# A two-part kernel with its MLP started later, its weight conversion moved with it, and a reordered first stage

## The chip, the cores and the metric

The kernel runs on one core of a Trainium2 chip. A core has five engines with a queue each, worked off in order: TensorE (PE; PEld are its weight loads), VectorE (DVE), ScalarE (ACT), GpSimd (POOL) and SyncE (SP, which here only issues transfers). The metric is the device time of one execution in microseconds, the median of several runs. The profile is of one further execution.

## The reference

Two computations in a row. The first is attention by random features, over 8 batches of 8 heads with 576 positions of 64 numbers:

```python
def phi(x):                                   # q and k, scaled by 64 ** -0.25
    proj = np.einsum('bhsd,md->bhsm', x, omega)          # omega: 128 x 64
    h = proj - np.sum(x * x, axis=-1, keepdims=True) / 2.0
    h = h - np.max(h, axis=-1, keepdims=True)
    return np.exp(h) / np.sqrt(m)
kv = np.einsum('bhsm,bhsd->bhmd', k_p, v)
num = np.einsum('bhsm,bhmd->bhsd', q_p, kv)
den = np.einsum('bhsm,bhm->bhs', q_p, np.sum(k_p, axis=2))[..., None] + 1e-06
```

Its result, as 4608 rows of 512, goes through a gated MLP, `silu(x @ w_gate) * (x @ w_val) @ w_out`, with 1536 inner columns. The three weights come in double precision (two 32-bit words a number).

## The kernel before, in words

Attention runs in 72 steps. A step takes two groups of 256 positions of a pair of heads: six steps with two groups of k (`AHEAD = 6`), then a q group and a k group each, and at the end two q groups. For a step, SP loads the two groups (`nat`), TensorE transposes them (`pt`), ScalarE copies them to SBUF (`x`, one copy a step, issued a step ahead), TensorE projects them on omega (`pp`), POOL squares them (`sq`), and VectorE forms the row sums of the squares and the row maxima of `pp` (`st`) and from both, in two small instructions, the bias of the exponential that ScalarE takes (`ph`). Groups of k are then multiplied with v into `kvacc`. Groups of q are transposed once more (`ptq`), multiplied with the sums (`po`), normalised (`xn`) and transposed (`xt`); ScalarE and VectorE split the result into a high and a low part, `xh` and `xl`, the MLP's input. `po`, `xt` and `ptq` share one PSUM buffer in most of the program, so that `xl` must be done before the next of them is written. `pt` takes PSUM from the MLP's pool of four buffers in the steps before `DENSE` and that single buffer from then on.

The MLP works on ten tiles of columns (512 wide, the first and last 256) and four sets of three blocks of 128 inner columns. A visit to one tile with one set is 36 gate matmuls (`g`), 36 value matmuls (`v`, both line 641), then 9 matmuls (`o`, line 650) for every 128 columns. All are products of high and low parts, three for one. Tiles are grouped in rounds, and the first round visits three tiles with all four sets.

A planner lays the MLP's work between the attention steps. `whole` tells after which step a tile is complete, `upper` and `lower` bound how many planned microseconds of MLP may and must be given out by a step, and `course` is the straightest line between. In step n the loop calls eleven pieces of attention work (`ORDER`) and after each gives out MLP matmuls (`give`) until `course` is met. What it writes down in this order, a scheduler then orders on each engine by its own estimate.

The weights are converted on the chip, in 36 pieces of 128 x 512 numbers. `convert_all` is a generator with seven operations a piece: ScalarE (L260), five on VectorE (L262, L264, L266, L268, L270), POOL's closing add (L272) with the store of the piece to a scratch tensor in HBM (`wscr`). `load_raw` (L225, L230) brings a piece's raw words into one of two buffers; a buffer is free again when the add has read it. The loop calls `tick` for one operation, as often as `want` says, which `marks` set: pairs of a step and a number of pieces. Before the change these are steps 0, 21, 23, 30, 33 and 35 with 0, 6, 9, 18, 27 and 36 pieces. The pieces of the first set stay in SBUF as high and low parts (`whi`, `wlo`), and later sets are read back from `wscr` and split when their set begins.

Of the kernel before, what the change touches and what calls it, by code (L numbers as in the profile page):

```python
# [16 lines left out]
ALU = mybir.AluOpType  # L17
AX = mybir.AxisListType
# [5 lines left out]
def kernel(  # L24
# [11 lines left out]
    nc = tc.nc  # L36
    B, H, S, D = q.shape
    M = omega.shape[0]
# [7 lines left out]
    NF = DF // P  # L46
# [3 lines left out]
    FA = 3  # L50
    NSET = NF // FA
# [8 lines left out]
    ROUNDS = [range(0, 3), range(3, 5), range(5, 7), range(7, 10)]  # L60
# [52 lines left out]
    AHEAD = 6  # L113
# [17 lines left out]
    def column(b, gr):  # L131
        return b * S + (S - RES if gr is None else gr[1])
# [50 lines left out]
    upper, lower = np.zeros(NN + 1), np.zeros(NN + 1)  # L183
    for n in range(NN + 1):
        vi = 0
        while vi < len(visits) and whole[visits[vi][0]] < n:
            vi += 1
        upper[n] = cum[vi] if n > whole[1] else 0.0
        lower[n] = max([0.0] + [cum[last_visit[j - NXB] + 1] for j in begun if j >= NXB and begun[j] <= n])
    lower = np.minimum(lower, upper)  # L190
    course = (lower + upper) / 2
# [23 lines left out]
    wscr = dram.tile([NF, 3, P, DM], F32, name="wscr")  # L215
    raws = {}

    def load_raw(n):
        if n < 3 * NF:
            f, i = divmod(n, 3) if n >= 3 * FA else (n % FA, n // FA)  # L220
            w = (wg32, wv32, wo32)[i]
            raw = att.tile([P, 2 * DM], I32, name=f"st{f}_{i}", tag="stw")
            raws[n] = f, i, raw
            if i < 2:
                nc.sync.dma_start(  # L225
                    raw.rearrange("p (c f) -> p c f", f=2 * P),
                    w[:, f * 2 * P : (f + 1) * 2 * P].rearrange("(c p) f -> p c f", p=P),
                )
            else:
                nc.sync.dma_start(raw, w[f * P : (f + 1) * P, :])  # L230
# [16 lines left out]
    def convert_all():  # L247


        load_raw(0)  # L250
        for n in range(3 * NF):
            load_raw(n + 1)
            f, i, raw = raws.pop(n)
            if f < FA:
                new_weights(f, i)
            u = moe.tile([P, DM], F32, name=f"wc{f}_{i}", tag="wraw", bufs=3)
            pairs = raw.rearrange("p (n t) -> p n t", t=2)
            low, r = pairs[:, :, 0], pairs[:, :, 1].bitcast(F32)
            ri, ui = r.bitcast(I32), u.bitcast(I32)
            nc.scalar.activation(u, r, AF.Abs)  # L260
            yield
            nc.vector.tensor_scalar(u, u, E_LO, E_HI, op0=ALU.max, op1=ALU.min)  # L262
# [3 lines left out]
            nc.vector.scalar_tensor_tensor(ri, ri, -0x40000000, ui, op0=ALU.bitwise_and, op1=ALU.bitwise_or)  # L266
# [3 lines left out]
            nc.vector.scalar_tensor_tensor(u, low.bitcast(U32), 2.0**-52, u, op0=ALU.mult, op1=ALU.mult)  # L270
            yield
            nc.gpsimd.tensor_tensor(u, r, u, op=ALU.add)  # L272
            if f < FA:
                split_piece(f, i, u)
            nc.sync.dma_start(wscr[f, i], u)
            converted.add((f, i))
            yield

# [43 lines left out]
    nats = {}  # L322
    busy = []

    def load_group(t, src, b, gr, v_):
        if gr is not None:
            pr, r = gr
            nc.sync.dma_start(
                t[:, :, :, 0:D],
                src[b, 2 * pr : 2 * pr + 2, r : r + G, :].rearrange("h (p c) d -> p c h d", c=CH),  # L330
            )
            return
        for c in range(CH):
            for j, pr in enumerate(pairs_of(gr)[c]):
                nc.sync.dma_start(
                    t[j * RES : (j + 1) * RES, 2 * c + j if v_ else c, :, 0:D],
                    src[b, 2 * pr : 2 * pr + 2, S - RES : S, :].rearrange("h p d -> p h d"),
                )

    def load(n):  # L340
        if n >= NS:
            return
        nats[n] = att.tile([P, 2, CH, 2, D], F32, name=f"nat{n}", tag="nat", bufs=3)
# [4 lines left out]
    def load_v(n):  # L348
        for i, b, g, gr in slots(n, "k"):
            rest = gr is None  # L350
            ts = (vtile, vrest)[rest]
            t = ts[nv[rest] % len(ts)]
            nv[rest] += 1
            assert t not in busy, "v's tile is still needed"
            busy.append(t)
            vrows[b, g] = t
            load_group(t, v, b, gr, True)

    box = {}
    sts = {}  # L360
# [38 lines left out]
    def st_max(n):  # L399
        if n >= NS:  # L400
            return
        st, sq, pp = sts[n]

        nc.vector.tensor_reduce(
            st[:, 0].rearrange("p i c h -> p (i c h)"),
            sq.rearrange("p i c h d -> p (i c h) d"),
            axis=AX.X,
            op=ALU.add,
        )
        for hh in range(2):  # L410
            nc.vector.tensor_reduce(st[:, 1, :, :, hh], pp[hh], axis=AX.X, op=ALU.max, negate=True)  # L411
        s0, s1, s2, s3 = (st[:, j].rearrange("p i c h -> p (i c h)") for j in range(4))
        nc.vector.scalar_tensor_tensor(s2, s0, SQC, s1, op0=ALU.mult, op1=ALU.add)
        nc.vector.scalar_tensor_tensor(s3, s0, -SQC, s2, op0=ALU.mult, op1=ALU.add)  # L414
        return True
# [405 lines left out]
```

## Time and profile before

| | |
|---|---|
| median of 3 runs | 1260.99 us (1258.11 to 1264.03) |
| the profiled execution | 1261.98 us, of it 1260.2 us span from the first to the last instruction |
| mean granted TensorE clock | 0.986 |
| moved by the transfers | 97.80 MB, mean 78 GB/s |

In the profile's rows a time is that from the span's start. A row of a stretch gives, engine by engine, the busy time and the number of instructions that began in it, then the clock that TensorE was granted (1.00 is full), the mean busy share of the 16 DMA engines and GB/s. A row of waits gives the waiting instruction, what ended its wait, the total, the number and the longest. In a row of instructions in order of time stand start, duration, engine, line, operation and tiles, and in brackets how long the engine had been idle and what ended that.

### The profile page before, as it was taken

The page shows a single profiled execution, that of the slowest core. Times are in us where ns is not written, and L with a number is a line of the kernel's source. Part 1 is how long each engine was busy: PE and PEld are TensorE (multiplying, and loading weights), DVE is VectorE, ACT ScalarE, POOL GpSimd, SP SyncE. Part 2 cuts the span into 40 slices and gives each one's busy share as a digit, 9 for nine tenths or more (in the row PEclk, how much of TensorE's full clock was granted, in tenths as well). Part 3 has the DMA queues.
Part 4 walks back from the last instruction along what each step waited for, and adds up shares of the span by engine and source line. Part 5 has one row for each costly group of instructions (what it writes and reads, how often), then busy time and mean ns, then how long its engine had stood idle before and what let it go on. Part 6 is the DMA issues. An engine that isn't in the chain of part 4 may idle for free.

```text
span 1260.2 us, 19027 instructions
## 1 busy us (share of the span) xinstructions
PE 1222.5 (97%) x7137; PEld 1004.1 (80%) x7137; DVE 526.1 (42%) x1080; ACT 632.5 (50%) x1368; POOL 506.2 (40%) x448
## 2 busy tenths in 40 slices
PE   6999999999899999999999999999999999999998
PEld 5888878888688878877777777877777778888887
DVE  4886795557732343334433433223343311121112
ACT  4887857564444645555556644853644323221211
POOL 3344444445442212644544334444654314242421
PEclk7999999999999999999999999999999999999999
DMA  6656555344521222222212221221211111010112
GB/s 161 152 139 154 141 146 172 106 137 122 159 67 52 61 65 60 76 67 62 65 51 67 68 59 38 64 65 45 52 50 30 39 25 50 25 51 25 51 30 55
DMA packets 157692, 97.80 MB, mean 78 GB/s; under 512 B 119680, under 2 KB 132000, under 8 KB 157600
## 3 DMA queue, kind: packets, MB, share of 16 engines
q1 hardware_dynamic: 157600, 96.59, 28.7%
q8 instruction: 56, 0.92, 0.3%
q14 instruction: 36, 0.29, 0.1%
HBM read 77.66 MB, written 18.89 MB: 77 GB/s over the span
## 4 chain that ended last, share of the span: by engine, by line
PE 67%; DVE 2%; POOL 2%; issue 1%; ACT 1%; DMA 0%; POOLq 0%; ACTq 0%
PE o L650 20%; PE g L641 19%; PE v L641 17%; PE pp L393 3%; PE kvacc L528 2%; PE ptq L552 2%; PE pt L370 2%; PE xt L607 1%; POOL jk L488 1%; PE po L569 1%; ACT ph L425 1%; DVE st L411 1%; DVE dj L492 0%; POOL wlo L243 0%; POOL hl L725 0%
## 5 line engine op out<-in xcount | busy, mean ns | idle before, releaser
L725 POOL TENSOR_TENSOR hl<-sl,hh 128x512 fp32r<-128x512 f32 (+1 forms) x120 | 145.3, 1211 | 223.0 <-ACT hh L724 222.9
L243 POOL TENSOR_TENSOR wlo<-wraw,whi 128x512 fp32r<-128x512 f32 x108 | 138.5, 1294 | 146.1 <-ACT whi L242 135.4
L425 ACT ACTIVATE ph<-pp,st 128x128 f32<-128x128 f32 x576 | 167.7, 387 | 57.7 <-DVE st L414 56.9
L641 PE MATMUL g<-xh,whi 128*128 128x512 f32 (+1 forms) x480 | 185.4, 387 | 0.0
L641 PE MATMUL v<-xh,whi 128*128 128x512 f32 (+1 forms) x480 | 184.3, 384 | 0.0
L641 PE MATMUL g<-xh,wlo 128*128 128x512 f32 (+1 forms) x480 | 179.8, 375 | 0.0
L641 PE MATMUL v<-xh,wlo 128*128 128x512 f32 (+1 forms) x480 | 179.3, 374 | 0.0
L641 PE MATMUL g<-xl,whi 128*128 128x512 f32 (+1 forms) x480 | 179.2, 373 | 0.0
L641 PE MATMUL v<-xl,whi 128*128 128x512 f32 (+1 forms) x480 | 178.5, 372 | 0.0
L650 PE MATMUL o<-whi,hh 128*128 128x512 f32 x432 | 176.5, 408 | 0.6 <-DVE sl L721 0.6
L650 PE MATMUL o<-whi,hl 128*128 128x512 f32 x432 | 169.9, 394 | 1.1 <-POOL hl L725 0.6
L650 PE MATMUL o<-wlo,hh 128*128 128x512 f32 x432 | 170.3, 394 | 0.0
L724 ACT CAST hh<-sl 128x512 fp32r<-128x512 f32 (+1 forms) x120 | 70.0, 583 | 174.5 <-DVE sl L721 174.1
L721 DVE TENSOR_TENSOR sl<-v,sl 128x512 f32<-128x512 f32 (+1 forms) x120 | 76.2, 635 | 172.2 <-PE v L641 167.9
L674 DVE TENSOR_TENSOR acc<-o,acc 128x512 f32<-128x512 f32 x108 | 74.1, 689 | 174.2 <-PE o L650 173.9
L377 POOL TENSOR_TENSOR sq<-nat 128x512 f32<-128x512 f32 x72 | 76.8, 1067 | 155.6 <-DMA nat<-in_k_dram 127.4
L411 DVE TENSOR_REDUCE st<-pp 128x4 f32<-128x512 f32 x144 | 93.5, 683 | 77.2 <-PE pp L393 77.1
L242 ACT CAST whi<-wraw 128x512 fp32r<-128x512 f32 x108 | 66.6, 622 | 97.3 <-PE v L641 55.3
L641 PEld LDWEIGHTS g<-xh,whi 128*128 128x128 f32 x480 | 91.6, 191 | 19.3 <-issue 4.2
L641 PEld LDWEIGHTS v<-xh,whi 128*128 128x128 f32 x480 | 91.0, 189 | 17.5 <-issue 2.7
L641 PEld LDWEIGHTS g<-xh,wlo 128*128 128x128 f32 x480 | 91.5, 191 | 15.9 <-issue 0.4
L641 PEld LDWEIGHTS v<-xh,wlo 128*128 128x128 f32 x480 | 91.0, 190 | 16.0 <-issue 0.5
(67 smaller groups left out, 1910.8 us busy)
## 6 DMA issues: line engine op xcount, KB each, us to landing
wraw<-wscr SPq DMA_DIRECT2D x108, 256.0 KB, 2.7
wscr<-wc SPq DMA_DIRECT2D x36, 256.0 KB, 2.3
out_dram<-acc SPq DMA_DIRECT2D x72, 128.0 KB, 2.3
nat<-in_k_dram SPq DMA_DIRECT2D x64, 128.0 KB, 3.2
v<-in_v_dram SPq DMA_DIRECT2D x64, 128.0 KB, 2.9
nat<-in_q_dram SPq DMA_DIRECT2D x64, 128.0 KB, 2.7
st<-in_moe_w_gate_dram SPq DMA_DIRECT2D x12, 512.0 KB, 4.2
st<-in_moe_w_val_dram SPq DMA_DIRECT2D x12, 512.0 KB, 4.6
```

The lines of the kernel that those rows point to most:

```text
L242: nc.scalar.copy(hi, raw)
L243: nc.gpsimd.tensor_tensor(lo, raw, hi.bitcast(F32), op=ALU.subtract)
L377: nc.gpsimd.tensor_tensor(sq, nat, nat, op=ALU.mult)
L393: nc.tensor.matmul(pp[hh][:, i, c, :], x[r, i, c * P : (c + 1) * P], omT[r], start=True, stop=True)
L411: nc.vector.tensor_reduce(st[:, 1, :, :, hh], pp[hh], axis=AX.X, op=ALU.max, negate=True)
L425: nc.scalar.activation(ph[:, c, hh * M : (hh + 1) * M], pp[hh][:, i, c, :], AF.Exp, bias=st[:, 3, i, c, hh : hh + 1], scale=1.0,)
L641: nc.tensor.matmul(ps, a_[:, ws], b_[:, c, :], start=n == 0, stop=n == 3 * NC - 1)
L650: nc.tensor.matmul(ps, a_[:, ts_], b_, start=first and n == 0, stop=last and n == 2)
L674: nc.vector.tensor_tensor(a_, po, a_, op=ALU.add)
L721: nc.vector.tensor_tensor(h, pv, h, op=ALU.mult)
L724: nc.scalar.copy(hh, h)
L725: nc.gpsimd.tensor_tensor(hl, h, hh.bitcast(F32), op=ALU.subtract)
```

## The change

Five edits are made. `upper` is zero up to `whole[2]` instead of `whole[1]`, so that the first MLP matmul comes in step 30 instead of step 21; `EARLY`, up to which odd steps' projections and all `ptq` use the MLP's PSUM pool, moves with it. `marks` become steps 0, 30 and 35 with 0, 9 and 36 pieces, and the order of the pieces is gates, values, outputs within each set. `wscr` is written by POOL instead of SP. Omega (one transfer instead of two) and the v of the first step are loaded from ScalarE's queue. VectorE's sums of squares stand behind the maxima, for the first six steps by a dependency that keeps the scheduler from turning them round again.

```diff
-        upper[n] = cum[vi] if n > whole[1] else 0.0
+        upper[n] = cum[vi] if n > whole[2] else 0.0
...
-    EARLY = whole[1]
+    EARLY = whole[2]
     clock = course + 4.0 * np.arange(NN + 1)
-    marks = [(0, 0.0), (EARLY, 2 * FA), (EARLY + 2, 3 * FA)]
-    for k_ in range(1, NSET):
-        at = int(np.searchsorted(course, cum[len(ROUNDS[0]) * k_ - 1]))
-        marks.append((max(at, marks[-1][0] + 1), 3 * FA * (k_ + 1)))
+    marks = [(0, 0.0), (EARLY, 3 * FA)]
+    marks.append((int(np.searchsorted(course, cum[len(ROUNDS[0]) * (NSET - 1) - 1])), 3 * NF))
     DENSE = marks[-1][0]
...
-            f, i = divmod(n, 3) if n >= 3 * FA else (n % FA, n // FA)
+            s_, m = divmod(n, 3 * FA)
+            f, i = s_ * FA + m % FA, m // FA
...
-            nc.sync.dma_start(wscr[f, i], u)
+            nc.gpsimd.dma_start(wscr[f, i], u)
...
-        for j in range(2):
-            nc.sync.dma_start(om2[:, j, :], omega)
+        nc.scalar.dma_start(om2, omega.rearrange("m (o d) -> m o d", o=1).broadcast_to([M, 2, D]))
...
-        nc.vector.tensor_reduce(
+        for hh in range(2):
+            top = nc.vector.tensor_reduce(st[:, 1, :, :, hh], pp[hh], axis=AX.X, op=ALU.max, negate=True)
+        sums = nc.vector.tensor_reduce(
             st[:, 0].rearrange("p i c h -> p (i c h)"),
             sq.rearrange("p i c h d -> p (i c h) d"),
             axis=AX.X,
             op=ALU.add,
         )
-        for hh in range(2):
-            nc.vector.tensor_reduce(st[:, 1, :, :, hh], pp[hh], axis=AX.X, op=ALU.max, negate=True)
+        if n < AHEAD:
+            tc.add_manual_dep(sums.ins, top.ins.name, ...)
...
-    for n in range(2):
-        load(n)
-        if n == 0:
-            setup_omega()
+    load(0)
+    setup_omega()
+    load(1)
     for n in range(LAV):
-        load_v(n)
+        load_v(n, nc.scalar)
```

How the instructions stand, at the places that the prediction uses. First VectorE at the program's start. `st` from `sq` is a sum of squares, `st` from `pp` a maximum, `st` from `st` one of the two small steps to the bias, and `wc` or `st_0` with 128x512 a conversion. Before:

```order
L404 TENSOR_REDUCE st_142<-sq_143 128x8
L404 TENSOR_REDUCE st_176<-sq_177 128x8
L404 TENSOR_REDUCE st_221<-sq_222 128x8
L411 TENSOR_REDUCE st_142<-pp_0_151 128x4
L411 TENSOR_REDUCE st_142<-pp_0_152 128x4
L404 TENSOR_REDUCE st_263<-sq_264 128x8
L413 SCALAR_TENSOR_TENSOR st_142<-st_142 128x8
L411 TENSOR_REDUCE st_176<-pp_1_203 128x4
L414 SCALAR_TENSOR_TENSOR st_142<-st_142 128x8
```

and after:

```order
L262 TENSOR_SCALAR wc_0_166<-wc_0_166 128x512
L264 TENSOR_SCALAR wc_0_166<-wc_0_166 128x512
L404 TENSOR_REDUCE st_141<-pp_0_150 128x4
L404 TENSOR_REDUCE st_141<-pp_0_151 128x4
L405 TENSOR_REDUCE st_141<-sq_142 128x8
L266 SCALAR_TENSOR_TENSOR st_0_160<-st_0_160,wc_0_166 128x512
L419 SCALAR_TENSOR_TENSOR st_141<-st_141 128x8
L404 TENSOR_REDUCE st_176<-pp_1_203 128x4
L420 SCALAR_TENSOR_TENSOR st_141<-st_141 128x8
```

The first maxima moved ahead of all sums, and the first conversion's first two operations moved ahead of the maxima. On TensorE the first MLP matmuls (`g`) stand before, in step 21, behind the transposes of step 19's exponentials:

```order
L370 MATMUL pt_1469<-ident,nat_1293 128x128
L552 MATMUL ptq_4_1496<-ident,ph_19_1430 128x128 x4
L528 MATMUL kvacc_1_1356<-v_99,ph_18_1366 128x65
L641 MATMUL g_0_1529<-xh_658,whi_0_165 128x256
L641 MATMUL g_0_1529<-xl_659,whi_0_165 128x256
```

and after, in step 30, behind that step's projections:

```order
L392 MATMUL pp_30_2181<-omT,x_2136 128x128
L392 MATMUL pp_30_2182<-omT,x_2136 128x128
L647 MATMUL g_0_2191<-xh_661,whi_0_164 128x256
L575 MATMUL po_2_2066<-kvr_1_1654,qt_2_2016 128x65 x4
L647 MATMUL g_0_2191<-xl_662,whi_0_164 128x256
```

All MLP matmuls moved nine steps back against the attention steps. Last, VectorE in step 34, around the `xl` that the transposes of step 35 wait for (`sl` is the MLP's product of gate and value, `acc` its sum). Before:

```order
L262 TENSOR_SCALAR wc_1_3962<-wc_1_3962 128x512
L721 TENSOR_TENSOR sl_6_3759<-v_6_3810,sl_6_3759 128x512
L414 SCALAR_TENSOR_TENSOR st_3571<-st_3571 128x8
L264 TENSOR_SCALAR wc_1_3962<-wc_1_3962 128x512
L266 SCALAR_TENSOR_TENSOR st_1_3907<-st_1_3907,wc_1_3962 128x512
L268 TENSOR_SCALAR wc_1_3962<-st_1_3907 128x512
L270 SCALAR_TENSOR_TENSOR wc_1_3962<-st_1_3907,wc_1_3962 128x512
L721 TENSOR_TENSOR sl_7_3761<-v_7_3832,sl_7_3761 128x512
L627 TENSOR_TENSOR xl_2245<-xt_7_3851,xh_2244 128x256
```

and after:

```order
L262 TENSOR_SCALAR wc_1_3809<-wc_1_3809 128x512
L264 TENSOR_SCALAR wc_1_3809<-wc_1_3809 128x512
L266 SCALAR_TENSOR_TENSOR st_1_3761<-st_1_3761,wc_1_3809 128x512
L268 TENSOR_SCALAR wc_1_3809<-st_1_3761 128x512
L270 SCALAR_TENSOR_TENSOR wc_1_3809<-st_1_3761,wc_1_3809 128x512
L262 TENSOR_SCALAR wc_2_3868<-wc_2_3868 128x512
L264 TENSOR_SCALAR wc_2_3868<-wc_2_3868 128x512
L266 SCALAR_TENSOR_TENSOR st_2_3807<-st_2_3807,wc_2_3868 128x512
L268 TENSOR_SCALAR wc_2_3868<-st_2_3807 128x512
L633 TENSOR_TENSOR xl_1977<-xt_7_3783,xh_1976 128x256
```

Two conversions, one of them up to its fourth operation, stand ahead of `xl` now, and no product of the MLP between them.

More of the change, by code (lines that the diff above doesn't have):

```diff
@@ L323, with load_group @@
     busy = []
-    def load_group(t, src, b, gr, v_):
+    def load_group(t, src, b, gr, v_, eng=nc.sync):
         if gr is not None:
             pr, r = gr
-            nc.sync.dma_start(
+            eng.dma_start(
                 t[:, :, :, 0:D],
@@ L346, in load, with load_v @@
                 load_group(nats[n][:, i], src, b, gr, False)
-    def load_v(n):
+    def load_v(n, eng=nc.sync):
         for i, b, g, gr in slots(n, "k"):
@@ L356, in load_v @@
             vrows[b, g] = t
-            load_group(t, v, b, gr, True)
+            load_group(t, v, b, gr, True, eng)
     box = {}
@@ L409, in st_max @@
         )
-        for hh in range(2):
-            nc.vector.tensor_reduce(st[:, 1, :, :, hh], pp[hh], axis=AX.X, op=ALU.max, negate=True)
+        if n < AHEAD:
+            tc.add_manual_dep(
+                sums.ins,
+                top.ins.name,
+                mybir.DependencyInfo(mybir.DependencyClass.NoSync, mybir.DependencyReason.DATA),
+                reason="the first maxima are waited for, these sums are not",
+            )
         s0, s1, s2, s3 = (st[:, j].rearrange("p i c h -> p (i c h)") for j in range(4))
```

## The prediction

> **What bounds the kernel now.** I read the page first, then the stretches between stages, then TensorE's waits in each stretch, and last the rows in order of time around the two worst places. From the page:
>
> ```profile
> PE 1222.5 (97%) x7137; PEld 1004.1 (80%) x7137; DVE 526.1 (42%) x1080; ACT 632.5 (50%) x1368; POOL 506.2 (40%) x448
> PEclk7999999999999999999999999999999999999999
> ```
>
> TensorE is busy 97% of the span, so no reordering saves work: only its idle time (1260.2 - 1222.5 = 37.7 us) and the time at a reduced clock can go. Where these lie shows when the matmuls are set against the time they need. The first fence has all instructions of some stretches (the columns are PE, PEld, DVE, ACT, POOL, then clock, DMA share, GB/s), the second only the gate and value matmuls (L641), the third only the down projection (L650).
>
> ```profile
> 0.00:31.00 31.00, 20.63 (x120) 18.16 (x121) 14.23 (x27) 12.52 (x34) 11.67 (x28) 0.72 0.67 163
> 20.00:30.00 10.00, 10.00 (x57) 9.31 (x58) 5.32 (x10) 5.36 (x17) 5.69 (x5) 0.50 0.73 184
> 46.00:101.00 55.00, 52.32 (x505) 46.91 (x504) 46.33 (x120) 46.01 (x143) 23.73 (x21) 1.00 0.60 148
> 306.50:344.50 38.00, 32.00 (x179) 27.07 (x178) 28.82 (x49) 15.67 (x30) 18.32 (x15) 0.96 0.45 135
> ```
> ```profile
> 106.50:197.00 90.50, 34.09 (x144) 23.47 (x144) 0.96 0.56 154
> 197.00:275.00 78.00, 53.30 (x252) 41.75 (x252) 1.00 0.42 128
> 275.00:306.50 31.50, 13.44 (x72) 11.12 (x72) 1.00 0.52 153
> 306.50:344.50 38.00, 22.78 (x109) 18.06 (x110) 0.96 0.45 135
> 344.50:408.50 64.00, 37.20 (x180) 29.61 (x178) 0.97 0.22 63
> 1100.00:1220.00 120.00, 83.56 (x432) 71.61 (x432) 1.00 0.12 34
> ```
> ```profile
> 106.50:197.00 90.50, 13.23 (x49) 8.64 (x50) 0.96 0.56 154
> 197.00:275.00 78.00, 15.56 (x66) 11.64 (x65) 1.00 0.42 128
> 275.00:306.50 31.50, 15.17 (x61) 10.76 (x60) 1.00 0.52 153
> 306.50:344.50 38.00, 6.36 (x27) 4.76 (x26) 0.96 0.45 135
> 344.50:408.50 64.00, 21.47 (x87) 15.89 (x88) 0.97 0.22 63
> 1100.00:1220.00 120.00, 38.39 (x167) 30.81 (x166) 1.00 0.12 34
> ```
> ```profile
> L641 PE MATMUL g<-xh,whi 128*128 128x256 f32 x24 | 6.8, 283 | 0.0
> 46.10 0.63 ACT L378 COPY x<-pt 128x512 f32<-128x512 f32 x1
> 101.24 0.63 ACT L378 COPY x<-pt 128x512 f32<-128x512 f32 x1
> 106.56 0.59 ACT L378 COPY x<-pt 128x512 f32<-128x512 f32 x1
> 197.12 0.58 ACT L378 COPY x<-pt 128x512 f32<-128x512 f32 x1
> ```
>
> The rate: 1100 to 1220 us holds MLP alone; six groups like the L641 row of the last fence, 144 matmuls, are 256 wide and count half. So 288 + 72 + 167 = 527 full matmuls in 120 us, 0.2277 us each. The step: one copy of x stands for one attention step; counted in order of time, those shown are of steps 8, 20, 21 and 30. Steps 8 to 20 hold no MLP: (101.24 - 46.10) / 12 = 4.6 us a step. What a stretch took beyond 0.2277 us a full matmul and 4.6 us a step is its excess (the 256-wide matmuls, 72, 72, 36, 36 and 72 of them, counted half):
>
> - steps 21 to 29 (106.5 to 197): 157 full matmuls, 35.7 us; 9 steps, 41.4; excess 13.4
> - 30 to 32: 282, 64.2; 13.8; excess 0
> - 33: 115, 26.2; 4.6; excess 0.7
> - 34: 118, 26.9; 4.6; excess 6.5
> - 35 and 36: 231, 52.6; 9.2; excess 2.2
>
> So the kernel loses 13.4 us where 37 us of MLP are strewn thinly over nine attention steps, and 6.5 us in step 34. TensorE's waits of these two stretches:
>
> ```profile
> PE po L569 <- DVE xl L627: 4.3, 5, 1.9
> PE pt L370 <- DVE xl L627: 6.0, 1, 6.0
> ```
>
> Both wait for VectorE's `xl`, which frees the single buffer of attention's PSUM. What stood ahead of `xl` at 342.7 us:
>
> ```profile
> 320.29 1.31 POOL L272 TENSOR_TENSOR wc<-st,wc 128x512 f32<-128x512 f32 x1 [1.14 <-issue]
> ...
> 342.31 1.30 POOL L272 TENSOR_TENSOR wc<-st,wc 128x512 f32<-128x512 f32 x1 [1.15 <-DVE wc L270]
> 332.04 0.67 ACT L260 ACTIVATE wc<-st 128x512 f32<-128x512 f32 x1 [4.79 <-DMA st<-in_moe_w_gate_dram]
> 336.46 0.16 DVE L413 SCALAR_TENSOR_TENSOR st<-st 128x8 f32<-128x8 f32 x1
> 339.36 0.69 DVE L266 SCALAR_TENSOR_TENSOR st<-st,wc 128x512 int32<-128x512 int32 x1
> 331.51 0.32 SPq L275 DMA_DIRECT2D wscr<-wc  x1
> ```
>
> Conversion pieces in a row. From the first to the fifth closing add it is 22.0 us, 5.5 us a piece: with two raw buffers the next raw load is issued only behind an add, and ScalarE waits for it (4.79 us). When more pieces than that stand ahead of `xl`, TensorE stops.
>
> **The change, part by part.**
>
> *MLP from step 30.* Steps 21 to 29 become like steps 8 to 20, at 4.6 us a step, with a conversion of 0.3 pieces a step as there. The 157 matmuls run later at the full rate and are covered by nothing less. Gain 13.4 us. Bound: were these steps 1.0 us slower (VectorE is busy 46.3 of 55 us there), 4.4.
>
> *Conversion later.* 27 pieces now fall on steps 30 to 34, 5.4 a step with 33 planned us of MLP; before, steps 30 to 32 had 3 pieces on 27 us and steps 33 and 34 had 4.5. The new pace, a piece per 6.1 planned us, is that of steps 33 and 34 (6.0). Those lost 0.7 and 6.5. Before step 35 the transposes of x take PSUM from the MLP's pool, so only `po` waits for `xl`, with more matmuls between; I take 1.5 us for each of steps 30 to 33, near step 33. Ends: 0 and 6.5. That is 6.0 against 0.7, a loss of 5.3. Step 34 still has conversions right ahead of its `xl`, so its 6.5 and the 2.2 behind it (the clock is 0.97 there) stay; at best they go.
>
> *The start.* SP issues one load after another; what carries the start:
>
> ```profile
> 12.23 1.19 SPq L225 DMA_DIRECT2D st<-in_moe_w_gate_dram  x2
> 16.75 0.66 ACT L260 ACTIVATE wc<-st 128x512 f32<-128x512 f32 x1 [4.32 <-DMA st<-in_moe_w_gate_dram]
> 12.49 0.69 DVE L404 TENSOR_REDUCE st<-sq 128x8 f32<-128x512 f32 x1 [3.42 <-POOL sq L377]
> 13.10 1.28 DVE L411 TENSOR_REDUCE st<-pp 128x4 f32<-128x512 f32 x2
> 17.31 4.22 ACT L425 ACTIVATE ph<-pp,st 128x128 f32<-128x128 f32 x16
> 17.44 0.43 DVE L262 TENSOR_SCALAR wc<-wc 128x512 f32<-128x512 f32 x1
> 17.71 2.48 PE L528 MATMUL kvacc<-v,ph 128*128 128x65 f32 x10 [3.02 <-ACT ph L425]
> 27.18 2.08 PE L393 MATMUL pp<-omT,x 64*128 64x128 f32 x16
> ```
>
> The first maxima (13.10) waited behind the third sum of squares (12.49). That goes, but VectorE's new order puts the first piece's L262 and L264 ahead of them. Raw weights: 17 issues stood ahead of the one at 12.23, 0.68 us each from 0.74; now 11, so about 8.2, and with the same 4.5 us to ScalarE, 12.7. Then 0.66 on ScalarE, twice 0.43, and up to the first bias, by the new order, two maxima 1.28, sums 0.69, L266 0.69, the first small step 0.16, a maximum 0.64, the second small step 0.16: the first exponentials at 17.9, against 17.31. They don't come sooner. Behind them TensorE is busy at half clock up to 31 us; the 16 matmuls at 27.18 (step 3's projections) now stand partly ahead of the first `kvacc`, in its wait: 2.1 us gained. Ends: a loss of 2 (the raw weights 4 us later than reckoned, which is nearly as late as before, and TensorE hiding half of that), a gain of 6.6 (the 13.2 us from 17.7 to 30.9 at full clock). Three loads issued by ScalarE cost nothing: its first work came at 5.57 us, behind omega. After that, sums behind maxima only trade places on VectorE.
>
> The page TensorE: Matmul & The Clock Gate of the Trainium skill (Part 1, What's actually happening) says that about 3.4 us of sustained work release the clock. The row of 20 to 30 us disagrees: 10.00 us busy, clock 0.50. By the page a gap less at the start would be worth most of the 6.6 us end.
>
> *wscr written from POOL.* 36 issues leave SP (0.32 us each, 11.5 in all) and go to POOL. SP gains no freedom: the next raw load waits there for the same add. On POOL the trace shows no issue; bounds are SP's 0.32 us and POOL's add of 1.30. Behind each issue wait `hl`, `wlo` and `sq`; POOL was busy 18.3 of 38 us in step 34, which covers 5.4 issues of 1.3. I take 0.5 us in all; ends -1 and 3. The Trainium skill's page DMA: Bandwidth & Descriptors (Issuing engines are not separate DMA queues) says issuing elsewhere only saves the sequencer's time; by it the start gains no transfer time, and the row of 0 to 31 us (163 GB/s, DMA share 0.67) shows no more.
>
> Sum: -13.4 + 5.3 - 2.1 + 0.5 = -9.7. The profiled execution took 1261.98 us (span 1260.2), 1.0 above the median of 1260.99: 1252.3 there, 1251.3 as a median; I say 1251.
>
> **The rivals.**
>
> - *Step 34's stall dissolves, or the clock returns early.* -8.7 us more (1242) or -4.5 more (1247). For: it is the only wait of this size in the trace, and the order around it is new. Against: conversions stand ahead of `xl` again.
> - *The conversions give the gain back.* If two of steps 30 to 33 lose 6.5 us as step 34 did, 10 us more: 1261. For: same pace, and the raw chain's 5.5 us a piece leaves little. All four: 1271, slower.
> - *Attention alone is not 4.6 us a step at 21 to 29.* With 5.6: 1260; the change then has moved work and saved little.
> - *POOL's issue is long.* In step 34 POOL had 19.7 us free, over 5.4 issues 3.6 us each. From there on POOL is the bound of steps 30 to 34: at 5 us an issue, 27 x 1.4 = 38 us more, 1289; it decides from 4.2 us (27 x 0.6 = 16, slower). Against: nothing in the trace issues that slowly.
>
> **How the numbers follow.** The forecast (1244 to 1254.7) 0.45; the better case 0.17; gain given back 0.18 and attention at 5.6 0.10, both within 0.5%; slower 0.10 (four bad steps or a long issue). Half a per cent, 1254.7 to 1267.3, is about what this kernel's runs tell from no change. Faster 0.62, same 0.28, slower 0.10. The ends: with step 34 cured and steps 30 to 33 at 0.7 each, 1261 - 13.4 - 2.1 - 8.7 + 2.1 + 0.5 = 1239; with nearly three of those steps at 6.5, 1251 + 14 = 1265.
>
> **What would show it.** Right: no MLP matmul before about 145 us, steps 21 to 29 at 4.6 us each; first exponentials still near 17.5 us; one wait of `pt` for `xl` of about 6 us in step 34. Wrong: several waits of 3 us or more for `xl` or `sl` between 145 and 340 us; POOL busy over 70% there; steps 21 to 29 at 5.5 us.

## The result, and the profile after

The changed kernel takes 1301.84 us (median of 4 runs, 1301.08 to 1307.33), the kernel before beside it 1260.16: a ratio of 1.0336, 95% interval 1.0298 to 1.0375. It is slower by 42 us where I had forecast 1251, and lies outside my range. The profiled execution took 1307.33 us, with a span of 1305.4 us against 1260.2. Where an execution lies over 1.5% above the fastest of its kernel it is left out of the ratios below; this concerns two of after_fill's four and one of no_vector_conversion's ten.

From the page:

```profile
PE 1249.6 (96%) x7137; PEld 1026.2 (79%) x7137; DVE 553.5 (42%) x1080; ACT 622.4 (48%) x1362; POOL 531.1 (41%) x484
PEclk7589899999889999999999999999999999999999
```

TensorE is busy 27 us longer with the same 7137 matmuls, and its clock is below 9 in several of the first twelve slices, where before only the first was. Stretches of the changed kernel, columns as in the prediction:

```profile
20.00:30.00 10.00, 10.00 (x48) 8.63 (x49) 7.95 (x14) 4.30 (x16) 5.93 (x5) 0.50 0.71 183
31.00:75.00 44.00, 43.27 (x235) 40.58 (x234) 24.41 (x47) 22.07 (x72) 15.75 (x15) 0.50 0.39 96
89.90:127.40 37.50, 36.73 (x351) 32.68 (x351) 34.04 (x88) 32.00 (x100) 21.91 (x20) 1.00 0.64 159
127.40:182.10 54.70, 48.47 (x393) 43.45 (x392) 45.99 (x112) 35.79 (x111) 21.16 (x21) 0.84 0.56 148
322.30:368.10 45.80, 32.63 (x174) 27.59 (x173) 32.03 (x49) 20.16 (x34) 26.34 (x24) 0.86 0.37 108
```
```profile
127.38 0.62 ACT L377 COPY x<-pt 128x512 f32<-128x512 f32 x1
182.11 0.65 ACT L377 COPY x<-pt 128x512 f32<-128x512 f32 x1
```

From 31 to 75 us TensorE is busy 43.27 of 44 us, at half clock. The clock record of the trace has one stretch at half from 13.8 to 75.3 us, 61.4 us long; before it was 17.1. The two copies of x are those of steps 21 and 30: step 21 comes 20.8 us later than before (106.6). Steps 21 to 29 now hold no MLP, as forecast, but take 6.08 us each, not 4.6, and 17.1 of their 54.7 us are at half clock.

Counted as in the prediction (0.2277 us a full matmul, 4.6 us a step), the excess of steps 30 to 34 is 21.3 us, against 8.1 before. Behind step 37's copy of x follow 861.8 us, before 851.8. So the 45.2 us more of span are: 20.8 up to step 21, nothing gained in steps 21 to 29, 13.2 in steps 30 to 34, 10.0 behind step 37, and some 1 between.

TensorE's waits from step 30 to step 36:

```profile
PE pt L369 <- DVE xl L633: 5.3, 1, 5.3
PE o L656 <- DVE sl L727: 4.7, 1, 4.7
PE g L647 <- DVE sl L727: 2.7, 1, 2.7
```

All lie in step 34. VectorE there, in order of time, and the first waiting matmul behind it:

```profile
321.89 0.43 DVE L262 TENSOR_SCALAR wc<-wc 128x512 f32<-128x512 f32 x1 [5.96 <-ACT wc L260]
322.35 0.43 DVE L264 TENSOR_SCALAR wc<-wc 128x512 int32<-128x512 int32 x1
322.81 1.67 DVE L266 SCALAR_TENSOR_TENSOR st<-st,wc 128x512 int32<-128x512 int32 x1
324.52 1.37 DVE L268 TENSOR_SCALAR wc<-st 128x512 int32<-128x512 int32 x1
325.93 0.69 DVE L270 SCALAR_TENSOR_TENSOR wc<-st,wc 128x512 f32<-128x512 uint32 x1
326.54 0.68 DVE L727 TENSOR_TENSOR sl<-v,sl 128x512 f32<-128x512 f32 x1
```
```profile
327.27 0.39 PE L647 MATMUL g<-xh,whi 128*128 128x256 f32 x1 [2.67 <-DVE sl L727]
```

A whole conversion stands ahead of the product `sl` in VectorE's queue. TensorE has nothing left from 324.6 us on and waits through the rest of it, 2.67 of its 4.7 us. The conversion came late itself: VectorE had been idle for 5.96 us until ScalarE's L260 was done. I had looked for such a wait at `xl` only.

The start of the changed kernel:

```profile
8.34 1.19 SPq L225 DMA_DIRECT2D st<-in_moe_w_gate_dram  x2
13.86 0.66 ACT L260 ACTIVATE wc<-st 128x512 f32<-128x512 f32 x1 [5.46 <-DMA st<-in_moe_w_gate_dram]
15.35 1.28 DVE L404 TENSOR_REDUCE st<-pp 128x4 f32<-128x512 f32 x2
15.98 0.57 ACT L377 COPY x<-pt 128x512 f32<-128x512 f32 x1
17.30 1.42 POOL L376 TENSOR_TENSOR sq<-nat 128x512 f32<-128x512 f32 x1 [9.09 <-DVE st L405]
19.45 1.40 ACT L431 ACTIVATE ph<-pp,st 128x128 f32<-128x128 f32 x5 [1.68 <-DVE st L420]
```

The raw words were issued where I had put them (8.2) and reached ScalarE 1.2 us later than I had reckoned (12.7). Two things were not in the reckoning: the copy of step 2's x (15.98, before 11.84) stands behind both openings of a conversion on ScalarE, and POOL's squares waited 9.09 us for VectorE to read the earlier ones. The first exponentials came at 19.45, not 17.9.

### The profile page after: what moved, and what is told of

Read it like the earlier page. It is cut to its first block, busy times and chain, and to the rows that moved or that the text cites. A ratio compares the mean times of both kernels' runs of the same rounds, so it can differ in the third digit from the quotient of the medians.

```text
span 1305.4 us, 19029 instructions
## 1 busy us (share of the span) xinstructions
PE 1249.6 (96%) x7137; PEld 1026.2 (79%) x7137; DVE 553.5 (42%) x1080; ACT 622.4 (48%) x1362; POOL 531.1 (41%) x484
## 4 chain that ended last, share of the span: by engine, by line
PE 77%; DVE 10%; ACT 4%; issue 4%; POOL 2%; DMA 2%; SPq 1%; ACTq 0%; POOLq 0%; DVEq 0%
PE o L656 19%; PE v L647 19%; PE g L647 19%; PE pp L392 6%; PE kvacc L534 6%; PE pt L369 3%; PE po L575 2%; PE ptq L558 2%; DVE st L404 2%; DVE st L420 1%; ACT ph L431 1%; PE xt L613 1%; DVE st L266 1%; DVE st L405 1%; DVE xl L633 1%
## 5 line engine op out<-in xcount | busy, mean ns | idle before, releaser
L730 ACT CAST hh<-sl 128x512 fp32r<-128x512 f32 (+1 forms) x120 | 69.7, 581 | 177.7 <-DVE sl L727 177.5
L392 PE MATMUL pp<-omT,x 64*128 64x128 f32 x1152 | 103.9, 310 | 2.2 <-ACT x L377 2.2
```

The costliest lines, as they stand in the source:

```text
L392: nc.tensor.matmul(pp[hh][:, i, c, :], x[r, i, c * P : (c + 1) * P], omT[r], start=True, stop=True)
L730: nc.scalar.copy(hh, h)
```

## The experiments

All times are device times; a ratio is to the kernel before, run beside it. Line numbers differ by a few between versions.

**Which edit costs what.** Four kernels: the start edits undone, `wscr` back on SP, the start edits alone, and the MLP's edits alone.

```diff
start_undone: changed kernel with omega and v from SP, sums ahead of maxima, no dependency
wscr_from_sp: changed kernel with
-            nc.gpsimd.dma_start(wscr[f, i], u)
+            nc.sync.dma_start(wscr[f, i], u)
start_only: kernel before with the edits to setup_omega, load_group, load_v, st_max, first loads
mlp_later_only: kernel before with the edits to upper, EARLY, marks and load_raw's order
```

> The changed kernel with its start as before: omega and v issued by SP, sums of squares ahead of the maxima, no dependency. The changed kernel takes 1302 us against 1260; of its 45 us more span, 20.8 stand before step 21, 14.4 in steps 21 to 36 and 10 behind. Theory S (the reordered start leaves TensorE too thinly fed to get its clock back): the first stretch at half clock shrinks from 61 us to about 17, step 21 comes near 107 us instead of 127, time 1275 to 1285. Theory W (wscr written from POOL): nothing of that, 1300. Theory M (MLP and conversion moved back): 1300 as well, with the loss in steps 30 to 36.

> The changed kernel with wscr written by SP again. Theory W: the store's longer landing (4.4 us against 2.3) and POOL's issues (0.6 us) hold ScalarE and the raw loads up; without them the 7.2 us wait of ScalarE for a wscr store in step 34 goes, time 1285 to 1292. Theory S: 1295 to 1302, first half-clock stretch still about 61 us. Theory M: 1300.

> The kernel before with the start edits alone (omega and v issued by ScalarE, sums behind the maxima). Theory S: half clock for 50 us or more from 14 us on, step 21 some 20 us late, time 1275 to 1290. Theories W and M: 1256 to 1262.

> The kernel before with the MLP from step 30, the new marks and the new order of pieces alone; start and wscr as before. Theory S with my sum of the prediction: steps 21 to 29 at 4.6 us, 1250 to 1255. Theory M: steps 30 to 36 lose what 21 to 29 gain and more, 1265 to 1280, with the first half-clock stretch still 17 us.

Four more split the start edits and take `wscr` by itself:

```diff
omega_only: kernel before with
-        for j in range(2):
-            nc.sync.dma_start(om2[:, j, :], omega)
+        nc.scalar.dma_start(om2, omega.rearrange("m (o d) -> m o d", o=1).broadcast_to([M, 2, D]))
...
+        load_v(n, nc.scalar)
sums_only: kernel before with the edit to st_max alone
wscr_only: kernel before with
+            nc.gpsimd.dma_start(wscr[f, i], u)
sums_six: kernel before with the edit to st_max for n < AHEAD, sums first for the others
```

> The kernel before with omega and the first v issued by ScalarE and the loads in the new order, sums still ahead of the maxima. In this version both first conversions' openings (ScalarE's L260) stand ahead of the copy of step 2's x, and L262 and L264 ahead of the first maxima. Theory S1 (that order is what starves TensorE at the start): half clock for 40 us or more from 14 us, step 21 some 15 us late, time 1273 to 1280, nothing lost behind step 37. Theory S2 (the sums behind the maxima do it, by holding POOL's squares and the loads of nat): 1258 to 1264.

> The kernel before with the sums of squares behind the maxima in all steps and the dependency in the first six, omega and v issued by SP. Theory S1: the start is as before or up to 4 us better, but the last 35 steps lose the 10 us that the changed kernel lost behind step 37: 1266 to 1270. Theory S2: half clock for 40 us or more, 1280 to 1285.

> The kernel before with wscr written from POOL alone. If the store from POOL costs of itself (ScalarE waits for a store to land before it may write the next piece), 1270 to 1290; if it costs only where conversions are dense, as in the version with the MLP from step 30, 1261 to 1268; by my prediction's 0.5 us, 1261.

> The kernel before with the sums behind the maxima in the first six steps alone, ahead of them from step 6 on. If the 10 us behind step 37 come from the order in the later steps, they are gone here: 1256 to 1262. If not, as sums_only.

And later the changed kernel without the MLP's edits (upper, EARLY, marks and pieces as before):

> The changed kernel with MLP, marks and order of pieces as before; the start edits and wscr from POOL stay. Alone, against 1260, start_only cost 22 us, wscr_only 9 and mlp_later_only 2.5. If the edits add up: 1290 to 1295 here, so that moving the MLP costs the changed kernel 7 to 12 us. If moving the MLP is what the others are paid for with: 1280 or less.

Measured, with the time at which step 21's x is copied, the time at half clock ahead of that, and what follows step 37's copy of x, from the profiled execution (the kernel before, run beside each group, had medians of 1259.8 to 1263.2 us):

| run | median, us | ratio (95% interval) | step 21 at | half clock before | behind step 37 |
|---|---|---|---|---|---|
| before | 1260 | 1 | 106.6 | 17.1 | 851.8 |
| changed | 1301.8 | 1.0336 (1.0298 to 1.0375) | 127.4 | 61.4 | 861.8 |
| start_undone | 1297.4 | 1.0246 (1.0192 to 1.0301) | 120.5 | 37.5 | 850.7 |
| wscr_from_sp | 1298.1 | 1.0280 (1.0230 to 1.0331) | 124.2 | 44.4 | 861.4 |
| mlp_undone | 1293.5 | 1.0256 (1.0194 to 1.0319) | 124.6 | 41.0 | 861.5 |
| start_only | 1285.4 | 1.0177 (1.0121 to 1.0233) | 122.4 | 44.4 | 861.5 |
| mlp_later_only | 1265.5 | 1.0020 (0.9981 to 1.0060) | 108.9 | 20.5 | 850.4 |
| omega_only | 1275.8 | 1.0118 (1.0095 to 1.0141) | 112.8 | 20.5 | 852.4 |
| sums_only | 1271.0 | 1.0083 (1.0061 to 1.0105) | 109.6 | 17.1 | 859.9 |
| wscr_only | 1269.1 | 1.0074 (1.0044 to 1.0103) | 109.3 | 17.1 | 850.4 |
| sums_six | 1266.7 | 1.0056 (1.0028 to 1.0083) | 115.1 | 34.1 | 850.2 |

No single edit is the culprit. Alone, the start costs 1.8%, `wscr` from POOL 0.7%, and the MLP's move nothing that can be told from zero; together 2.7% if they multiplied, against 3.4% measured. Undoing any one gives back less than 1%. start_undone missed theory S by 12 us: it lost the clock again at 46.6 us for 17.1 us and at 128.5 us for 23.9. wscr_from_sp came to the time of S, not of W, but its first stretch at half clock is 27.3 us and not 61. mlp_undone is where the edits add up. mlp_later_only lies at the lower end of theory M, sums_only 1 us above the range of S1, and wscr_only between two of its forecasts. omega_only came to the time of S1 but not by its way, with only 20.5 us at half clock. sums_six lost no time behind step 37, as expected, but its trace has 17.1 us more at half clock, from 97 us on, and it came out above its forecast. The executions of one version can differ by more than these effects: two of start_only's took 1280 us and two 1291 and 1292, the last of them the profiled one, while omega_only's profile is of its shortest (1270.9 us).

*The 10 us behind step 37* come from the order of the sums in the later steps. The eight traces with the sums behind the maxima in all steps show 859.9 to 861.9 us there, the twelve others 850.1 to 852.5, sums_six among them. VectorE and POOL at one such place in sums_only, from the last maximum on, VectorE at one in sums_six, and then the second small step over the whole stretch behind step 37, first sums_only, then sums_six:

```profile
501.54 0.68 DVE L405 TENSOR_REDUCE st<-pp 128x4 f32<-128x512 f32 x1
502.13 0.68 DVE L406 TENSOR_REDUCE st<-sq 128x8 f32<-128x512 f32 x1
502.73 0.16 DVE L420 SCALAR_TENSOR_TENSOR st<-st 128x8 f32<-128x8 f32 x1
502.89 1.04 POOL L377 TENSOR_TENSOR sq<-nat 128x512 f32<-128x512 f32 x1 [0.26 <-DVE st L420]
502.92 1.04 DVE L421 SCALAR_TENSOR_TENSOR st<-st 128x8 f32<-128x8 f32 x1
504.05 0.37 ACT L432 ACTIVATE ph<-pp,st 128x128 f32<-128x128 f32 x1 [2.79 <-DVE st L421]
```
```profile
515.99 1.29 DVE L415 TENSOR_REDUCE st<-pp 128x4 f32<-128x512 f32 x2 [0.20 <-PE pp L393]
517.53 0.15 DVE L425 SCALAR_TENSOR_TENSOR st<-st 128x8 f32<-128x8 f32 x1
517.72 0.17 DVE L426 SCALAR_TENSOR_TENSOR st<-st 128x8 f32<-128x8 f32 x1
```
```profile
L421 DVE SCALAR_TENSOR_TENSOR st<-st 128x8 f32<-128x8 f32 x35 | 30.4, 869 | 1.1
```
```profile
L426 DVE SCALAR_TENSOR_TENSOR st<-st 128x8 f32<-128x8 f32 x35 | 6.9, 197 | 1.2
```

Two things make the bias later. The sum stood ahead of the maxima, where VectorE waited for the projections anyway; now it stands between the last maximum and the small steps and takes 0.6 us there. And the sums, read last now, free a buffer of squares just ahead of the small steps. POOL starts the next squares at once, and the small step that starts beside it lasts 1.04 us, as long as POOL's instruction, instead of 0.16 (on average 869 ns instead of 197). Over the 35 steps behind step 37, the bias is ready 1.70 us after the last maximum in sums_only and 0.59 us after it in sums_six; each of the two makes about half of this. How the 10 us divide between them no run separates. The page SBUF — State Buffer of the Trainium skill (Who interferes with whom) says that a VectorE instruction with two SBUF inputs contends with a GpSimd instruction that reads SBUF, over ports that one of them holds exclusively. The trace agrees: the small step reads two SBUF operands, while the sums, with one, last 676 ns in one version and 686 in the other.

*wscr from POOL.* In wscr_only the stores land later, and SP waits for them where it reads them back (L294); first the stores with their median landing, before and in wscr_only, then SP's waits from 60 to 360 us in the same order:

```profile
wscr<-wc SPq DMA_DIRECT2D x36, 256.0 KB, 2.3
```
```profile
wscr<-wc POOLq DMA_DIRECT2D x36, 256.0 KB, 4.5
```
```profile
SPq L294 <- DMA wscr<-wc: 11.4, 11, 2.2
```
```profile
SPq L294 <- DMA wscr<-wc: 43.1, 13, 4.8
```

What is queued behind such a read on SP are raw words: ScalarE's L260 waited 23.3 us for them there, 14.4 before. POOL's issue itself is short (36 of 0.58 us). But the landing cannot be the whole of it. The first of these reads is issued at 199.8 us before and at 200.7 us in wscr_only, and by then wscr_only has lost most of its time: the copy of step 30's x comes at 202.2 us instead of 197.1, which is 5.1 us of the 6.4 by which the two spans differ. Where these 5.1 us come from, POOL's issues between its add and `wlo` or SP's changed order of loads, no run separates.

**Is the conversions' place what starves the start?** In the versions with omega on ScalarE, the scheduler puts conversion openings ahead of step 2's x and of the first maxima. Two kernels take them away, one from omega_only, one from the changed kernel:

```diff
-    marks = [(0, 0.0), (EARLY, ...
+    marks = [(0, 0.0), (3, 0.0), (EARLY, ...
```

> omega_only (1275.8 us) with no conversion before step 3, so that no conversion's opening stands ahead of step 2's x, of the first maxima or of the first exponentials. Theory S1: the start is no longer starved, steps 0 to 7 take 47 us instead of 51 and steps 8 to 20 no longer than before, 1259 to 1267. If the loads issued by ScalarE cost of themselves: 1273 to 1279.

> The changed kernel (1302 us) with no conversion before step 3; all five edits stay. Theory S1 (the conversions' openings ahead of step 2's x and the first exponentials lose the clock there): step 21 comes at 108 to 115 us instead of 127, and the time is 1284 to 1292. If the clock is lost for another reason (half clock came back by chance in before_fill): step 21 at 120 us or later, 1296 to 1306.

omega_late_conv: 1263.9 us, 1.0011 (0.9998 to 1.0025); of omega_only's 1.2% a tenth of a per cent is left, and the interval takes in 1. late_conversion: 1304.5 us, 1.0341 (1.0286 to 1.0395), step 21 at 125.6 us, 47.8 us at half clock before it. So the conversions' place explains omega_only's loss, though the two profiles, of which omega_only's is of its shortest run, show only 2.0 us of it ahead of step 21. Theory S1 falls in the changed kernel, which lost its clock at 15.8 us although its first conversion came only at 34.3, and again at 46.5.

**Is it TensorE's density?** One kernel writes the transposes of steps 2 to 5 three times over, two put 32 transposes of the identity behind those of step 2, where TensorE waits.

```diff
after_dense (changed kernel):
-        for i in range(2):
+        for i in [0, 1] * (3 if 2 <= n <= 5 else 1):
before_fill, after_fill:
+        if n == 2:
+            dm = ps_att("dm", [P, 2, G])
+            for j in range(32):
+                d_ = nc.tensor.transpose(dm[...], ident, ident)   # behind the last transpose of step 2
```

> The changed kernel (1302 us) with the transposes of steps 2 to 5 written three times over into the same PSUM tile: 32 more TensorE instructions of 128x128, 7 us at full clock and 14 us at half, with no other work. Theory D (TensorE stays at half clock for 61 us because the mix of small matmuls in a 3.4 us window does too little, not because it waits): the first half-clock stretch ends by 45 us instead of 75 us and the time is 1285 to 1298 in spite of the added work. If the clock does not care what TensorE does: the stretch is as long or longer and the time 1306 to 1316.

> The kernel before with 32 transposes of the identity into an unused PSUM tile, right behind the transposes of step 2, where TensorE waits about 6 us for the first exponentials. Theory D (the clock is lost because TensorE does too little in the 3.4 us window ahead of 13.9 us, and half clock is what the start costs): no half-clock stretch at 14 us, the work from 17 to 31 us up to 6.6 us sooner, 1252 to 1258. If the clock is not the cause: 1260 to 1266, or the stretch is there all the same.

> The changed kernel with the same 32 transposes at the same place; there TensorE waits 4.4 us for nat and again for the exponentials. Theory D: the 61 us at half clock from 14 us shrink to under 20 us, step 21 comes by 112 us instead of 127, 1284 to 1292. If half clock only goes along with the late conversion openings: 1299 to 1306 with step 21 still near 127 us.

after_dense: 1304.1 us, 1.0331 (1.0298 to 1.0365), between the two forecasts. The first stretch is broken up (6.8 us at 21.5, 17.1 at 35.1), step 13 comes 10 us sooner than in the changed kernel, and a new stretch at 96.6 us takes that back; steps 21 to 29, at full clock all through, take 5.03 us each. before_fill: 1272.6 us, 1.0108 (1.0079 to 1.0136). after_fill: 1292.2, 1304.7 and twice 1319.0 us, a ratio of 1.0312 (1.0264 to 1.0360) for the two shorter, and its profile is of one of the longer, so that its trace shows what can happen, not what the ratio stands for. In both the clock stayed up past 13.9 us, as theory D said, but the 32 transposes had ended by 15.3 and 15.8 us, the wait went on, and the clock fell one or two windows later (19.4 and 18.9 us) and again at 36.4 and 49.6. Filling this one gap was no cure.

All twenty traces together say more than these three runs. In them the clock changes only at steps of 3.41 us, which I call windows. For each window of the first 400 us I added up the columns that its matmuls stream (the last number of their shape), those of `pp`, which has 64 rows, counted half:

| clock in the window | columns | windows | clock in the next window |
|---|---|---|---|
| half, TensorE busy over 99% | under 1545 | 145 | full in 3 |
| half, TensorE busy over 99% | 1545 or more | 92 | full in 87 |
| full | under 1540 | 81 | half in 79 |
| full | 1540 or more | 1879 | half in 16 |

The columns tell the next window's clock where busy time does not: 147 of the 237 busy windows were followed by half clock. The table leaves out 72 windows at half clock in which TensorE was not busy throughout. Of these 16 held 1540 columns or more, and only 5 of the 16 were followed by full clock; and in all 16 windows that lost the clock above the bound TensorE was busy for under 65%. Both exceptions nearly vanish when the MLP's columns are counted half too: a bound of 1540 then tells 304 of all 309 windows at half clock right, and 1956 of 1960 at full. Weights and bound were chosen on these same windows; no run was made to test them.

Attention alone does 2430 columns a window at full clock (before, 46 to 106 us) and 1303 at half (changed kernel, 24 to 72 us), although TensorE is busy throughout. So a lost clock tends to stay lost, until a window happens to hold more. Both kernels lose it at the same place, 13.9 and 13.8 us, behind windows of 1396 and 1083 columns; the return differs. Before, the window at 27.5 us holds 1849 columns and the clock is back at 30.9 us. In the changed kernel none holds more than 1530 until that at 71.9 us, with 1742, and the clock is back at 75.3 us. The MLP alone does 7643 columns a window at full clock (before, 1100 to 1220 us), 3821 when counted half, so that half clock does not keep itself up there; from step 30 to 400 us a lost clock is back after one to three windows. Half clock costs about half its time: over the 17 traces without added matmuls, the time of step 21 is 101.2 + 0.48 times the half clock before it (correlation 0.92, largest deviation 7 us).

**What steps 30 to 34 lose.** Four kernels on the kernel before with the MLP from step 30: the old pace and order of conversion; three raw buffers; without VectorE's part of the later conversions; 16 pieces by step 30.

```diff
mlp_old_marks:
+    marks = [(0, 0.0), (21, 2 * FA), (23, 3 * FA), (30, 6 * FA), (33, 9 * FA), (35, 3 * NF)]
three_raw:
-            raw = att.tile([P, 2 * DM], I32, name=f"st{f}_{i}", tag="stw")
+            raw = att.tile([P, 2 * DM], I32, name=f"st{f}_{i}", tag="stw", bufs=3)
...
-            load_raw(n + 1)
+            load_raw(n + 2)
no_vector_conversion: the five nc.vector operations of convert_all under
+            if f < FA:
even_conversion:
-    marks = [(0, 0.0), (EARLY, 3 * FA)]
+    marks = [(0, 0.0), (EARLY, 16)]
```

> The kernel before with the MLP from step 30, but the conversion at its old pace (0, 6, 9, 18, 27, 36 pieces at steps 0, 21, 23, 30, 33, 35) and in its old order. My prediction put the 13.4 us that steps 21 to 29 lost down to MLP work strewn among attention. Theory P (that was right): these steps take 4.6 to 4.9 us each here and steps 30 to 34 lose 8 us as before, 1250 to 1254. Theory Q (the nine extra pieces converted in these steps were the loss): they take 5.7 us or more each without any MLP, 1259 to 1267.

> mlp_later_only (1265.5 us) with three raw buffers instead of two and the raw words loaded two pieces ahead. In mlp_later_only steps 30 to 34 lose 22 us beyond 0.2277 us a full matmul and 4.6 us a step. Theory R (the chain from add to load to ScalarE, 5.5 us a piece, sets the pace and makes xl late): the loss falls to 8 to 14 us, 1251 to 1259. Theory V (VectorE's own row of conversions ahead of xl does it, whenever the words come): 1262 to 1268, step 34's wait of pt for xl still above 6 us.

> mlp_later_only (1265.5 us) without VectorE's five operations for the 27 pieces of sets 1 to 3 (the weights of these sets are then not the reference's); raw loads, ScalarE's and POOL's operations and the stores stay. Theory V (VectorE's conversion rows stand ahead of sl and xl): the 22 us that steps 30 to 34 lose fall to 5 to 10, 1248 to 1255. If ScalarE, POOL or the transfers set the pace there: 1261 to 1268.

> mlp_later_only with 16 instead of 9 pieces converted by step 30, evenly over the first 30 steps, so that 20 instead of 27 stand in steps 30 to 34. If VectorE's slack in the attention steps hides the seven pieces: the 22 us lost in steps 30 to 34 fall to about 15 and the time is 1256 to 1260. If VectorE has no slack there (it is busy 46 of 55 us), the attention steps lose what is gained: 1262 to 1272, with more half clock ahead of step 30.

| run | median, us | ratio (95% interval) | pieces in steps 30 to 34 | their excess, us | steps 21 to 29 less their MLP matmuls, us each (half clock) |
|---|---|---|---|---|---|
| before | 1260 | 1 | 18 | 8.1 | 6.09 (6.8) |
| changed | 1301.8 | 1.0336 | 27 | 21.3 | 6.08 (17.1) |
| mlp_later_only | 1265.5 | 1.0020 | 27 | 21.9 | 4.92 (0) |
| three_raw | 1271.5 | 1.0071 (1.0041 to 1.0101) | 27 | 21.9 | 5.46 (6.8) |
| no_vector_conversion | 1257.8 | 0.9987 (0.9961 to 1.0014) | 27 | 7.6 | 5.25 (0) |
| mlp_old_marks | 1283.9 | 1.0159 (1.0125 to 1.0193) | 18 | 13.2 | 7.21 (28.0) |
| even_conversion | 1269.5 | 1.0067 (1.0041 to 1.0094) | 20 | 13.2 | 5.14 (0) |

Theory R falls: with a third raw buffer the excess is the same. Theory V holds in that VectorE's queue does it: without its operations 14 of the 22 us go. (Of the time only 8 us go, fewer than forecast, and three_raw, at 1271.5 us, lies above V's range.) Whether it is the length of these operations or that they wait in the queue for ScalarE's L260, with `sl` and `xl` behind them, the runs do not separate, as taking the operations out removes both. VectorE's waits for L260 from step 30 to 34, in mlp_later_only and in three_raw:

```profile
DVE wc L261 <- ACT wc L259: 31.6, 12, 8.3
```
```profile
DVE wc L262 <- ACT wc L260: 30.7, 10, 8.3
```

TensorE's waits from step 30 to 34, in mlp_later_only and in no_vector_conversion:

```profile
PE o L649 <- DVE sl L720: 7.3, 2, 5.0
PE pt L369 <- DVE xl L626: 4.7, 1, 4.7
```
```profile
PE pt L373 <- DVE xl L630: 2.8, 1, 2.8
PE po L572 <- DVE xl L630: 2.5, 2, 1.5
```

The waits for `sl` are gone and that for `xl` is shorter. Fewer pieces there lose less (13.2 us with 20), but what moves ahead costs as much: even_conversion reaches step 21 at 121.6 us instead of 108.9. Theory Q fits mlp_old_marks in direction only: 28 us at half clock hide what nine extra conversions alone would cost in steps 21 to 29.

No version beat the kernel before.

## Why the prediction was wrong, point by point

The step that failed first is the start: it stands in the sum with -2.1 us and at worst +2, and measured +20.8 by step 21, with TensorE's clock at half for 61.4 us ahead of it instead of 17.1; at the 0.48 us for each us at half clock of the 17 traces, that is 21. The MLP's gain (-13.4) came to nothing, the later conversion (+5.3) cost 13.2, and the order of the sums (nothing) cost 10.0. Term by term:

- **The MLP from step 30, -13.4 us.** The move is worth 10.5 us in steps 21 to 29 where the clock holds (mlp_later_only, 4.92 us a step), somewhat less than taken, with the conversions moved too. In the changed kernel nothing of it is left. There ScalarE waited for raw words with `xh` queued behind, `xl` and `po` waited in turn, and the clock fell at 157 us:

```profile
154.05 0.66 ACT L260 ACTIVATE wc<-st 128x512 f32<-128x512 f32 x1 [2.07 <-DMA st<-in_moe_w_gate_dram]
154.61 0.36 ACT L632 CAST xh<-xt 128x256 fp32r<-128x256 f32 x1
155.00 0.42 DVE L633 TENSOR_TENSOR xl<-xt,xh 128x256 fp32r<-128x256 f32 x1 [1.94 <-ACT xh L632]
155.48 1.11 PE L575 MATMUL po<-kvr,qt 128*128 128x65 f32 x8 [1.69 <-DVE xl L633]
```

  The window of this gap of 1.7 us, from 153.8 us on, holds 1211 columns, and 10.2 us at half clock followed. "Covered by nothing less" is what failed in this term: before, the strewn MLP had brought a lost clock back after one window, at 116.3 and at 177.7 us (in start_only, at 190.0 us, after four).
- **Later conversion, +5.3 us.** Mis-sized: 13.8 us (21.9 against 8.1 in mlp_later_only, with 11.6 us at half clock in these steps against 3.0). I took the old step 33 as the model for four steps, though the matmuls also wait for `sl`, which the prediction's sum does not have. This is the rival in which the conversions give the gain back, 1261; alone it came out at 1265.5, no change.
- **The start, -2.1 us, ends -6.6 and +2.** This term failed worst: +15.8 us by step 21 in the profile of start_only, +20.8 in the changed kernel, and still +13.9 with the start undone. The durations were nearly right (exponentials 1.5 us late). The sum took it that the clock would come back at about 31 us as before; what it left out is that at half clock attention alone stays below the bound, so that the order of TensorE's work decides over tens of us. I had the row that shows it (10.00 us busy at 0.50) and used it only against the rule of the page TensorE: Matmul & The Clock Gate of the Trainium skill (Part 1, What's actually happening). By that rule one busy window of about 3.4 us releases the clock. If busy means the busy time of the trace, the traces disagree: 147 of 237 windows busy throughout did not release it.
- **"Sums behind maxima only trade places", 0 us.** 10 us: the sum now delays the bias itself, and POOL's squares beside the small step delay it as much again.
- **wscr from POOL, +0.5 us, ends -1 and 3.** 9 us alone. I priced the issue, which at 0.58 us lies inside my bounds, and not the landing and who reads back; but most of the loss in wscr_only lies ahead of the first read-back, and its cause stays open.
- **What would show it.** "Wrong" named several waits of 3 us or more for `xl` or `sl` up to 340 us and steps 21 to 29 at 5.5 us. The second came (6.08 us); of the first there is one, for `sl` (4.7 us), beside another of 2.7. The step 34 wait of `pt` for `xl`, which "right" put at about 6 us, is 5.3.

What stays open: which of the edits' changes of order keeps the windows of the changed kernel below the bound for 61 us. Each remedy at the start moved the stretches about; why a given version escapes is not settled beyond the count of columns. A version that takes away the start's gap as a whole wasn't tried.

## What to carry to other kernels

Before moving heavy matmuls out of a thin stage, count the array work per clock window that is left: if half of it is below the bound, a gap that loses the clock there can be paid for many times over. Look at what each reordering releases (a buffer, and with it another engine's instruction beside yours), not only at the order on its own engine. And when a store changes its queue, look at its landing and at who reads it back, besides the issue; here that still left most of the loss unexplained.

## What the runs showed of the hardware

- TensorE's clock: in windows of 3.41 us, a bound of about 1540 columns, with 64-row matmuls and the MLP's (of type fp32r in the rows that write `xh` and `xl`) counted half, tells the next window's clock right for 304 of 309 windows at half clock and 1956 of 1960 at full, in the first 400 us of the twenty traces that it was fitted to.
- A VectorE instruction of 128x8 lasts 0.16 us alone and 1.04 us when POOL's 1.04 us instruction has started 0.03 us before it; conversions lengthen likewise (L266 1.67 us at 322.81 beside POOL's `wlo`, L262 2.58 us at 329.97; 0.69 and 0.43 alone).
- The same 256 KB store lands 2.3 us after issue from SP and 4.5 from POOL, whose issue takes 0.58 us.
